# Linear attention with a gated convolution: q of four batches loaded in rows and in channels, with one set of PSUM tiles

## The chip, the cores and the metric

The kernel runs on one core of a Trainium2 chip. The metric is the device time in microseconds; it was measured in three runs of the kernel before. A profiled execution of the same program gives the trace. In the profile TensorE is called PE (its weight loads PEld), VectorE is DVE, ScalarE is ACT, GpSimd is POOL, and SyncE is SP; SP issues all DMAs of this kernel.

## The reference

There are 8 batches, 8 heads, 576 tokens and a head size of 64, so 512 channels; all data is float32.

```python
q_s = softmax(q, axis=-1)              # over the 64 channels of a head
k_s = softmax(k, axis=2)               # over the 576 tokens
kv  = einsum('bhsd,bhse->bhde', k_s, v)
x   = einsum('bhsd,bhde->bhse', q_s, kv)   # heads side by side: (8, 576, 512)

gate = sigmoid(sum over j of conv_w[j] * x shifted by 4 - j tokens)   # 5 taps
out  = (gate * (x @ w_val)) @ w_out
```

Both sums of a softmax get 1e-9 added before the division.

## The kernel before

The work goes batch by batch, and batches overlap. Channels are cut in 4 blocks of 128 (`NB`), and a block holds two heads. The tokens are 4 parts of 128 (`MAIN`, 512) and a tail of 64, which two batches share in one tile.

A list of named steps, `ORDER`, is written out by hand, as "name, batch, block or part, engine" (`a` ScalarE, `v` VectorE, `p` GpSimd). Each engine runs its instructions in the order of this list; nothing is reordered. A tile of a pool with n buffers waits for the release of an older one. The steps of one batch are:

- q: `load_q` brings the tokens on partitions, `q_max`, `q_sub`, `q_exp`, `q_sum` and `q_mul` make the softmax along the free axis. `q_turn` turns two blocks of 128 channels on TensorE (8 transposes of 128x128, line 445), `q_turned` copies them to SBUF; `tail_turn` and `tail_turned` do this for the shared tail (line 459). So q stands with its channels on partitions.
- k: `load_km`, `k_peak`, `k_row` (to DRAM) and `k_spread` (from DRAM to all partitions) give the maximum, `k_sub` and `k_exp` the exponential. Batches 0 and 1 take another way (`load_kc`, `k_top`, `k_raise`, `k_turn`).
- `kv` is the product over tokens (line 423), `kv_norm` divides by the sum of k, which comes from a column of ones at v.
- `attend b g` makes x for blocks 2g and 2g + 1 in two PSUM tiles (line 478), in pieces of 288, 224 and 64 tokens.
- `first` and four `tap` make the gate's sum from x in PSUM, on VectorE or on ScalarE and GpSimd together; `sigmoid` ends it. `x_high` and `x_low` split x into two rounded parts.
- `value b m` multiplies by w_val (24 matmuls of three terms: line 521), `gated` multiplies by the gate, `g_high` and `g_low` split again, `project b n` multiplies by w_out (line 521 again), `store` copies out of PSUM and sends it off.

The weights come as pairs of 32-bit words and are rebuilt at the start, in slabs: `load_words`, `part`, `field`, `scaled`, `signed`, `joined`, `w_high`, `w_low`. Slab i holds 128 output columns for all rows of the matrix, 0 to 3 of w_val, 4 to 7 of w_out, 8 the taps.

PSUM has two sets of two tiles, each of two banks: the tag `x` (for `attend`, `q_turn`, `q_lift`, `q_peak`) and the tag `mm` (the rest). The turned q has a tile of its own (`qT`), q itself two.

Of the kernel before, what the change touches and what calls it, by code (L numbers as in the profile page):

```python
# [23 lines left out]
KM = 3  # L24
EPS = 1e-9
MOST = 122880 - 2.0 ** -7
# [5 lines left out]
    load_q 0 0 2, load_words 1, q_max 0 0 2, load_ident, q_peak 0 0 2, load_words 8, part 8 a, field 1, scaled 1 a,  # L32
    signed 1, part 1 v, joined 1 p, w_high 1 p, field 8, scaled 8 a, q_top 0 0 2 a, load_kc 0 2, k_top 0 2,
    k_raise 0 2, q_lift 0 0, q_minus 0 0, w_low 1 p, load_q 0 2 5, q_lift 0 1, load_kc 0 1, q_max 0 2 5, k_top 0 1,
    load_kc 0 3, k_top 0 3, q_raise 0 0, k_raise 0 3, signed 8, q_peak 0 2 5, q_top 0 2 5 a, load_words 3, part 3 a,
    field 3, scaled 3 p, load_kc 0 0, k_top 0 0, load_q 1, signed 3, joined 3 p, k_turn 0 1, k_raise 0 0, q_minus 0 1,
    k_turned 0 1 a, q_raise 0 1, q_max 1, k_raise 0 1, load_words 4, field 4, w_high 3 p, scaled 4 a, load_kc 1 1,
    k_top 1 1, q_lift 0 2, q_minus 0 2, load_kc 1 0, k_top 1 0, k_turn 0 0, q_raise 0 2, k_raise 1 1, k_tail_turn 0,
    k_tail_turned 0 a, load_v 0, q_sum 0, signed 4, q_exps 1 1 p, q_exps 1 0 p, k_turned 0 0 a, q_exps 1 3 p,
    load_words 0, k_raise 1 0, field 0, q_exps 1 2 p, q_mul 0 1 v, scaled 0 p, joined 8 p, load_kc 1 2, k_top 1 2,  # L40
    load_words 2, q_sum 1, kv 0, field 2, q_mul 0 0 a, q_mul 0 2 a, q_mul 0 3 p, part 0 a, q_turn 0 0, q_turned 0 0 a,
    q_turn 0 1, q_turned 0 1 a, q_mul 0 4 p, kv_norm 0 a, load_kc 1 3, k_top 1 3, scaled 2 p, signed 2, tail_turn 0,
    tail_turned 0 a, attend 0 0, w_low 3 v, signed 0, part 2 a, joined 0 p, w_high 0 p, load_words 5, field 5,
    load_v 1, w_low 0 p, first 0 1 a, tap 0 1 3 v, first 0 0 a, x_high 0 0 a, k_raise 1 2, k_raise 1 3, k_turn 1 0,
    tap 0 1 2 v, k_turned 1 0 a, tap 0 0 3 v, load_words 6, tap 0 1 1 v, k_turn 1 1, tap 0 0 2 v, x_low 0 0,
    q_mul 1 2 p, k_turned 1 1 a, tap 0 0 1 v, tap 0 0 0 v, part 4 a, load_words 7, joined 2 p, joined 4 p,
    k_tail_turn 1, k_tail_turned 1 a, x_high 0 1 a, x_low 0 1, kv 1, tap 0 1 0 v, scaled 5 a, signed 5, kv_norm 1 v,
    sigmoid 0 0, q_mul 1 1 p, attend 0 1, load_k 3, part 5 a, x_high 0 2 a, joined 5 p, load_q 2, x_low 0 2, field 7,
    x_high 0 3 a, x_low 0 3, value 0 0, w_high 2 a, w_low 2 p, value 0 2, first 0 2 a, tap 0 2 3 v, w_high 4 a,
    w_low 4 p, load_kt 2, tap 0 2 2 v, q_mul 1 0 p, first 0 3 a, tap 0 3 3 v, load_km 2 1, gated 0 0, tap 0 2 1 a,  # L50
    load_km 2 2, scaled 7 a, tap 0 3 2 v, tap 0 3 1 v, tap 0 3 0 v, signed 7, k_peak 2 1, load_km 2 3, tap 0 2 0 a,
    q_mul 1 3 a, sigmoid 0 1, g_high 0 0 a, g_low 0 0 p, value 0 1, q_turn 1 0, k_peak 2 2, sigmoid 0 2, q_turn 1 1,
    load_km 2 0, gated 0 2, w_high 5 a, w_low 5 p, q_turned 1 0 a, g_high 0 2 a, part 6 a, g_low 0 2 p, gated 0 1,
    field 6, g_high 0 1 a, g_low 0 1 p, q_turned 1 1 a, load_k 2, load_v 2, value 0 3, q_max 2, q_sub 2 0 p,
    k_peak 2 3, k_peak 2 0, k_row 2, sigmoid 0 3, gated 0 3, attend 1 0, x_high 1 0 a, first 1 0 a, g_high 0 3 a,
    x_high 1 1 a, scaled 6 p, k_spread 2, first 1 1 a, signed 6, g_low 0 3 v, joined 6 p, w_high 6 a, q_sub 2 3 p,
    project 0 1, store 0 1 a, project 0 0, x_low 1 0, tap 1 1 3 v, w_low 6 p, project 0 2, tap 1 0 3 v, tap 1 1 2 v,
    tap 1 1 1 v, load_km 3 3, tap 1 0 2 v, part 7 a, tap 1 0 1 v, joined 7 p, tap 1 1 0 a, w_high 7 a, w_low 7 p,
    tap 1 0 0 v, sigmoid 1 0, x_low 1 1, load_km 3 2, store 0 2 a, load_km 3 0, k_peak 3 3, k_peak 3 2, store 0 0 a,
    attend 1 1, x_high 1 2 a, x_low 1 2, load_km 3 1, x_high 1 3 a, x_low 1 3, load_q 3, first 1 2 a, tap 1 2 3 v,  # L60
    tap 1 2 2 v, tap 1 2 1 v, q_sub 2 1 p, tap 1 2 0 v, first 1 3 a, q_sub 2 4 p, tap 1 3 3 v, k_peak 3 1, k_peak 3 0,
    project 0 3, store 0 3 a, k_sub 2 2 p, value 1 0, gated 1 0, k_sub 2 1 p, q_sub 2 2 p, sigmoid 1 1, q_exp 2,
    g_high 1 0 a, q_sum 2, k_sub 2 0 p, k_sub 2 4 p, k_sub 2 3 p, k_exp 2, value 1 1, gated 1 1, value 1 2, load_v 4,
    q_mul 2 0 a, q_mul 2 4 p, q_mul 2 1 p, tap 1 3 2 v, tap 1 3 1 v, load_km 4 0, tap 1 3 0 v, k_row 3, k_spread 3,
    kv 2, kv_norm 2 v, g_low 1 0 v, g_high 1 1 v, q_mul 2 2 a, g_low 1 1 v, sigmoid 1 2, q_mul 2 3 p, q_turn 2 0,
    q_turned 2 0 a, gated 1 2, g_high 1 2 p, load_km 4 1, k_peak 4 1, g_low 1 2 p, q_turn 2 1, q_turned 2 1 a,
    k_sub 3 2 p, load_km 4 2, load_v 3, k_sub 3 1 v, k_peak 4 2, value 1 3, sigmoid 1 3, gated 1 3, load_km 5 2,
    tail_turn 2, tail_turned 2 a, attend 2 0, g_high 1 3 a, g_low 1 3 p, load_km 4 3, x_high 2 1 a, k_sub 3 3 p,
    first 2 1 a, x_high 2 0 a, k_sub 3 0 p, q_max 3, q_sub 3 3 p, k_peak 4 3, first 2 0 a, tap 2 0 3 v, k_sub 3 4 p,
    tap 2 0 2 a, tap 2 0 1 a, tap 2 1 3 v, q_sub 3 0 p, x_low 2 1, project 1 3, store 1 3 v, x_low 2 0, k_exp 3,  # L70
    tap 2 1 2 v, tap 2 1 1 v, tap 2 1 0 v, tap 2 0 0 a, k_peak 4 0, k_row 4, k_spread 4, q_sub 3 1 p, project 1 0,
    load_km 5 3, store 1 0 v, project 1 1, store 1 1 a, q_sub 3 2 p, attend 2 1, x_high 2 3 a, x_low 2 3,
    x_high 2 2 a, load_k 4, first 2 2 a, tap 2 2 3 a, q_exp 3, first 2 3 v, k_peak 5 2, tap 2 3 3 v, kv 3,
    tap 2 3 2 v, tap 2 3 1 a, tap 2 3 0 a, load_q 4, kv_norm 3 v, project 1 2, store 1 2 a, x_low 2 2, q_sum 3,
    q_mul 3 3 p, q_mul 3 1 p, value 2 0, tap 2 2 2 v, sigmoid 2 0, tap 2 2 1 v, gated 2 0, g_high 2 0 v, load_km 5 1,
    q_mul 3 2 a, value 2 1, sigmoid 2 1, gated 2 1, load_km 6 3, q_mul 3 0 p, g_low 2 0 v, tap 2 2 0 a, q_turn 3 0,
    sigmoid 2 2, g_high 2 1 p, g_low 2 1 p, q_max 4, q_sub 4 2 p, q_sub 4 0 p, q_turn 3 1, q_turned 3 1 a, value 2 2,
    q_sub 4 4 p, gated 2 2, g_high 2 2 p, g_low 2 2 p, q_turned 3 0 a, attend 3 0, x_high 3 1 a, x_high 3 0 v,
    first 3 0 a, k_peak 5 1, load_q 5, load_k 6, tap 3 0 3 v, load_km 7 0, x_low 3 0, x_low 3 1, sigmoid 2 3,
    value 2 3, gated 2 3, g_high 2 3 v, first 3 1 a, g_low 2 3 v, k_peak 6 3, load_kt 4, k_sub 4 4 p, tap 3 0 2 a,  # L80
    tap 3 0 1 a, q_sub 4 1 p, tap 3 0 0 a, tap 3 1 3 v, k_sub 4 3 p, tap 3 1 2 v, tap 3 1 1 v, tap 3 1 0 v,
    load_km 5 0, project 2 0, store 2 0 v, q_sub 4 3 v, project 2 1, attend 3 1, first 3 2 v, first 3 3 v,
    x_high 3 2 a, k_peak 5 3, tap 3 3 3 v, store 2 1 a, load_km 6 2, tap 3 2 3 v, project 2 2, project 2 3,
    sigmoid 3 1, tap 3 2 2 v, k_sub 4 1 v, tap 3 2 1 v, x_low 3 2, x_high 3 3 a, x_low 3 3, store 2 2 a, k_sub 4 2 p,
    k_sub 4 0 v, q_exp 4, value 3 1, tap 3 2 0 a, q_sum 4, q_mul 4 3 p, q_mul 4 2 p, store 2 3 a, q_mul 4 0 p,
    k_exp 4, gated 3 1, sigmoid 3 0, value 3 0, k_peak 6 2, tap 3 3 2 a, gated 3 0, g_high 3 0 a, tap 3 3 1 a,
    k_peak 5 0, k_row 5, g_high 3 1 a, value 3 2, g_low 3 1 p, q_max 5, q_sub 5 1 p, tap 3 3 0 v, q_sub 5 2 p,
    q_mul 4 1 a, sigmoid 3 2, gated 3 2, load_km 6 0, k_peak 6 0, kv 4, kv_norm 4 v, q_turn 4 0, g_low 3 0 v,
    sigmoid 3 3, q_turn 4 1, q_turned 4 1 v, q_sub 5 3 p, k_spread 5, q_mul 4 4 p, value 3 3, gated 3 3,
    q_turned 4 0 a, q_sub 5 0 p, g_high 3 3 p, g_high 3 2 a, g_low 3 3 p, g_low 3 2 v, tail_turn 4, tail_turned 4 a,  # L90
# [549 lines left out]
```

## Time and profile before

| what | us |
| --- | --- |
| median of 3 runs | 311.24 |
| lowest and highest run | 308.35, 311.43 |
| the profiled execution | 309.28 |
| its span, first to last instruction | 307.5 |
| TensorE busy | 287.0 |
| VectorE busy | 247.3 |
| ScalarE busy | 207.4 |
| GpSimd busy | 187.7 |

The profile's page gives the busy time of each engine, its groups of instructions by line and what ended the idle time ahead of them, the chain of work that ended last, and the transfers with their time from issue to landing. Times within the execution count from the start of the span.

### The profile page before, as it was taken

To read this page: it belongs to the slowest core of one execution; us is meant where nothing else is said; L and a number is where in the kernel's file an instruction comes from. 1 tells how busy PE (TensorE), PEld (TensorE's weight loads), DVE (VectorE), ACT (ScalarE), POOL (GpSimd) and SP (SyncE) were. 2 spreads that over 40 slices of the span, in tenths; PEclk is the share of its full clock that TensorE was granted. 3 is DMA by queue.
4 is the path that set the end of the run, shared out by engine and by line. 5 is a ranking of instruction groups with operands and counts; after the bars stand their busy time and mean duration, and the time that the engine had idled before them with its cause. 6 is when DMAs were issued, how large, how long until landed. Compare 5 with 4: busy or idle time off the path is not lost.

```text
span 307.5 us, 6827 instructions
## 1 busy us (share of the span) xinstructions
PE 287.0 (93%) x2769; PEld 266.5 (87%) x2769; DVE 247.3 (80%) x338; ACT 207.4 (67%) x338; POOL 187.7 (61%) x163
## 2 busy tenths in 40 slices
...
GB/s 216 394 387 381 117 335 80 221 211 285 350 180 164 41 263 337 312 87 117 45 215 319 288 123 226 173 175 108 45 3 19 100 40 2 13 104 41 0 46 109
DMA packets 20527, 51.28 MB, mean 167 GB/s; under 512 B 2832, under 2 KB 7312, under 8 KB 17808
## 3 DMA queue, kind: packets, MB, share of 16 engines
...
## 4 chain that ended last, share of the span: by engine, by line
PE 59%; DMA 13%; ACT 8%; DVE 7%; POOL 6%; issue 4%; SPq 1%; ACTq 0%; DVEq 0%; POOLq 0%
PE out L521 21%; PE val L521 21%; PE kv L423 5%; DMA q<-in_q_tail 4%; PE x L478 3%; DMA km<-in_k_strided 3%; PE qTps L445 3%; DMA v<-in_v 3%; DMA out<-o 2%; DVE gate L503 2%; PE qlps L401 2%; DMA ident<-in_ident 2%; POOL q L346 2%; POOL gl L550 2%; PE qlps L406 2%
## 5 line engine op out<-in xcount | busy, mean ns | idle before, releaser
L521 PE MATMUL val<-x,w_val_hi 128*128 128x288 f32 x512 | 88.9, 295 | 0.0
L507 POOL TENSOR_TENSOR gate<-gate,far 128x572 f32<-128x572 f32 (+3 forms) x38 | 51.0, 1345 | 47.2 <-ACT far L506 46.2
L521 PEld LDWEIGHTS val<-x,w_val_hi 128*128 128x128 f32 x512 | 75.4, 188 | 0.0
L503 DVE SCALAR_TENSOR_TENSOR gate<-x,cw,gate 128x574 f32<-128x574 f32 (+3 forms) x90 | 71.7, 809 | 3.5 <-ACT gate L491 2.0
L521 PE MATMUL out<-gh,w_out_lo 128*128 128x288 f32 x256 | 56.9, 301 | 0.0
L521 PE MATMUL out<-gl,w_out_hi 128*128 128x288 f32 x256 | 56.0, 297 | 0.9 <-DVE gl L550 0.6
L521 PE MATMUL val<-x,w_val_lo 128*128 128x288 f32 x256 | 56.2, 301 | 0.0
L521 PE MATMUL out<-gh,w_out_hi 128*128 128x288 f32 x256 | 55.4, 295 | 0.0
L521 PEld LDWEIGHTS out<-gl,w_out_hi 128*128 128x128 f32 x256 | 41.4, 188 | 2.0 <-DVE gl L550 1.2
L521 PEld LDWEIGHTS out<-gh,w_out_lo 128*128 128x128 f32 x256 | 41.1, 188 | 1.0 <-DVE o L158 0.3
L506 ACT ACTIVATE far<-x,cw 128x572 f32<-128x572 f32 (+3 forms) x38 | 27.2, 736 | 21.8 <-DVE gate L503 16.5
L521 PEld LDWEIGHTS out<-gh,w_out_hi 128*128 128x128 f32 x256 | 41.6, 188 | 0.0
L521 PEld LDWEIGHTS val<-x,w_val_lo 128*128 128x128 f32 x256 | 40.9, 188 | 0.5
L542 DVE TENSOR_TENSOR g<-val,gate 128x576 f32<-128x576 f32 x32 | 23.9, 749 | 14.5 <-PE val L521 8.4
L156 ACT COPY o<-out 128x576 f32<-128x576 f32 (+1 forms) x23 | 14.2, 618 | 21.2 <-PE out L521 18.5
L510 ACT ACTIVATE gate<-gate 128x576 f32<-128x576 f32 x32 | 21.4, 684 | 10.6 <-DVE gate L503 6.9
L379 POOL TENSOR_TENSOR q<-q,qs 128x512 f32<-128x512 f32 x23 | 23.6, 1045 | 8.0 <-DVE qs L359 8.0
L497 DVE TENSOR_TENSOR x<-x,x 128x576 fp32r<-128x576 f32 x32 | 23.4, 751 | 4.9 <-ACT x L156 3.7
L342 DVE TENSOR_REDUCE qm<-q 128x32 f32<-128x2048 f32 (+3 forms) x9 | 20.5, 2279 | 8.1 <-DMA q<-in_q 4.8
L423 PE MATMUL kv<-v,k 128*64 128x65 f32 x512 | 22.0, 238 | 4.0 <-ACT k L156 2.7
L491 ACT ACTIVATE gate<-x,cw 128x576 f32<-128x576 f32 x24 | 17.7, 747 | 11.0 <-DVE x L497 3.9
L346 POOL TENSOR_TENSOR q<-q,qm 128x512 f32<-128x512 f32 x22 | 23.7, 1089 | 2.3 <-DVE qm L342 2.3
...
## 6 DMA issues: line engine op xcount, KB each, us to landing
...
v<-in_v SPq DMA_DIRECT2D x8, 1040.0 KB, 9.9
q<-in_q SPq DMA_DIRECT2D x7, 1024.0 KB, 7.7
...
k<-in_k SPq DMA_DIRECT2D x6, 1024.0 KB, 7.7
...
words<-in_w_val SPq DMA_DIRECT2D x4, 512.0 KB, 8.1
words<-in_w_out SPq DMA_DIRECT2D x4, 512.0 KB, 9.0
```

The lines of the kernel that those rows point to most:

```text
L342: nc.vector.tensor_reduce(out=T["qm", b][:, cs], in_=qq, axis=AX.X, op=ALU.max, negate=(b == 1))
L346: engine(e).tensor_sub(qq, qq, T["qm", b][:, cs].unsqueeze(2).broadcast_to([P, H, D]))
L379: engine(e).tensor_mul(qq, qq, s.unsqueeze(2).broadcast_to([P, H, D]))
L423: nc.tensor.matmul(acc[h * D:(h + 1) * D, p, :], T["k", b][:, c, cs] if c < 4 else ktz[b % 2][:, cs], T["v", b][:, c, hd] if c < 4 else T[ ...
L491: nc.scalar.activation(a, x, AF.Copy, scale=w)
L497: nc.vector.tensor_sub(xl, T["x", b, p], T["xh", b, p].bitcast(F32))
L503: nc.vector.scalar_tensor_tensor(out=a, in0=x, scalar=w, in1=a, op0=ALU.mult, op1=ALU.add)
L506: nc.scalar.activation(part, x, AF.Copy, scale=w)
L507: nc.gpsimd.tensor_add(a, a, part)
L510: nc.scalar.activation(T["gate", b, p], T["gate", b, p], AF.Sigmoid)
L521: nc.tensor.matmul(ps[:, cs], a[:, kb, ms], z[kb][:, cs], start=(kb == 0 and i == 0), stop=(kb == NB - 1 and i == 2),)
L542: nc.vector.tensor_mul(T["g", b, m], T["val", b, m], T["gate", b, m])
```

## The change

For batches 4 to 7, q is loaded twice. `load_qa` brings it in rows: a partition holds 36 rows (`ROWS`) of 64 channels, of one head each. `qa_max`, `qa_sub` (four pieces of 9 rows), `qa_exp` and `qa_sum` make the sum of the exponentials there, `qa_log` its logarithm plus the maximum. `q_row` sends these to DRAM, and two `q_spread` bring each head's row back to the 64 partitions of its channels. `load_qT` brings q with its channels on partitions; `q_add` subtracts the row, one block at a time, and `q_up` takes the exponential of two blocks. `q_turn`, `tail_turn` and `q_mul` go for these batches. `attend` takes their tokens in two pieces of 288 (`b >= EARLY`).

All q tiles, turned or not, share one tag of four buffers (`Q`). The turned tail takes a buffer of the tag `o`. PSUM has one set of four tiles. w_val is loaded by rows (slab i holds 128 rows of the matrix, all 512 columns), while w_out keeps its slabs of columns. `value` may come in two halves of the sum over blocks, which the four of batch 0 do. The step `signed` is cut in `shifted` and `signed`, and `field` may go to GpSimd. `ORDER` is new throughout, with other engines for some steps: 97 `tap` on VectorE and 31 on ScalarE with GpSimd (90 and 38 before).

```diff
-    psum = ctx.enter_context(tc.tile_pool(name="psum", bufs=2, space=PSUM))
-    def bank(name, tag="mm"):
-        return psum.tile([P, 2 * 512], F32, tag=tag, name=name)
+    psum = ctx.enter_context(tc.tile_pool(name="psum", bufs=4, space=PSUM))
+    def bank(name):
+        return psum.tile([P, 2 * 512], F32, tag="ps", name=name)
...
+    def q_tile(name):
+        return big.tile([P, 5 * C], F32, tag="q", name=name, bufs=Q)
...
+        elif i < NB:
+            nc.sync.dma_start(out=T["words", i], in_=w_val[:, i].rearrange("p (c t) -> p c t", t=2))
...
+    def load_qa(b):
+        T["qa", b] = q_tile(f"qa_{b}")[:, :ROWS * D]
+        nc.sync.dma_start(out=T["qa", b], in_=qa[b])
+    def load_qT(b):
+        nc.sync.dma_start(out=q_across(b), in_=qc[b])
+    def qa_max(b):
+        T["qm", b] = small.tile([P, 5 * H], F32, tag="qm", name=f"qm_{b}")[:, :ROWS]
+        nc.vector.tensor_reduce(out=T["qm", b], in_=by_row(b), axis=AX.X, op=ALU.max)
+    def qa_sub(b, i, e="p"):
+        ts = slice(ROWS // 4 * i, ROWS // 4 * (i + 1))
+        x = by_row(b)[:, ts]
+        engine(e).tensor_sub(x, x, T["qm", b][:, ts].unsqueeze(2).broadcast_to([P, ROWS // 4, D]))
+    def qa_exp(b):
+        nc.scalar.activation(T["qa", b], T["qa", b], AF.Exp)
+    def qa_sum(b):
+        s = T["qs", b] = small.tile([P, 5 * H], F32, tag="qs", name=f"qs_{b}")[:, :ROWS]
+        nc.vector.tensor_reduce(out=s, in_=by_row(b), axis=AX.X, op=ALU.add)
+        nc.vector.tensor_scalar_add(s, s, EPS)
+    def qa_log(b):
+        s = T["qs", b]
+        nc.scalar.activation(s, s, AF.Ln)
+        nc.vector.tensor_add(s, s, T["qm", b])
+    def q_row(b):
+        t = T["qrow", b] = rowpool.tile([H * S], F32, tag=f"qrow{b}", name=f"qrow{b}")
+        nc.sync.dma_start(out=t.rearrange("(p j) -> p j", j=ROWS), in_=T["qs", b])
+    def q_spread(b, half):
+        if ("qw", b) not in T:
+            T["qw", b] = q_tile(f"qw_{b}")[:, :NB * S].rearrange("p (n s) -> p n s", n=NB)
+        to = T["qw", b][half * D:(half + 1) * D].rearrange("p n s -> p (n s)")
+        r = T["qrow", b].rearrange("(o t m) -> o t m", o=1, t=2)[:, half]
+        nc.sync.dma_start(out=to, in_=r.broadcast_to([D, NB * S]))
+    def q_add(b, n, e="p"):
+        x = T["qT", b][:, n]
+        engine(e).tensor_sub(x, x, T["qw", b][:, n])
+    def q_up(b, g):
+        x = T["qT", b][:, 2 * g:2 * g + 2]
+        nc.scalar.activation(x, x, AF.Exp)
...
-        for t0, t1 in ((0, HALF), (HALF, MAIN), (MAIN, S)):
+        for t0, t1 in ((0, HALF), (HALF, MAIN), (MAIN, S)) if b < EARLY else ((0, HALF), (HALF, S)):
...
-    def value(b, m):
-        T["val", b, m] = halved_bank(f"val_{b}_{m}")
-        split_product(T["val", b, m], W[0], blocks("xh", b), blocks("xl", b), m)
+    def value(b, m, g="a"):
+        if ("val", b, m) not in T:
+            T["val", b, m] = halved_bank(f"val_{b}_{m}")
+        ks = range(NB) if g == "a" else (2 * g, 2 * g + 1)
+        z = [[T.get((x, b, k)) for k in range(NB)] for x in ("xh", "xl")]
+        split_product(T["val", b, m], W[0], *z, m, ks=ks)
```

From the new `ORDER`: its start, the first `value`, the chain of q for batch 7, and the end.

```diff
+    load_q 0 0 2, load_words 8, load_ident, q_lift 0 0, load_words 1, part 1 a, q_max 0 0 2, field 1 v, scaled 1 a,
+    field 8 p, scaled 8 p, load_words 3, field 3 v, scaled 3 a, shifted 1 v, part 8 a, signed 1, shifted 3 v,
...
+    load_v 1, kv 1, kv_norm 1 a, load_k 3, tap 0 1 2 v, tap 0 1 1 v, tap 0 1 0 v, attend 0 1, x_high 0 2 a,
+    first 0 2 a, x_low 0 2, load_q 3, tap 0 2 3 v, load_kt 2, first 0 3 a, x_high 0 3 a, x_low 0 3, w_low 0 p,
+    w_low 2 p, value 0 0 0, value 0 0 1, w_low 4 p, tap 0 2 2 v, tap 0 3 3 v, load_q 2, part 5 a, tap 0 2 1 v,
...
+    gated 5 3, g_high 5 3 v, g_low 5 3 v, g_high 5 0 p, g_low 5 0 p, k_spread 7, qa_log 7, q_row 7, kv 6, kv_norm 6 v,
+    q_up 6 0, project 5 3, q_spread 7 0, k_sub 7 0 v, attend 6 0, x_high 6 1 a, k_sub 7 1 v, first 6 1 a, project 5 2,
+    store 5 3 a, project 5 0, k_sub 7 4 v, first 6 0 v, tap 6 0 3 v, k_sub 7 3 v, k_sub 7 2 v, tap 6 0 2 a, k_exp 7,
+    tap 6 1 3 v, tap 6 1 2 a, store 5 2 v, q_add 6 3 v, q_spread 7 1, tap 6 0 1 v, kv 7, q_add 6 2 v, x_high 6 0 v,
+    q_up 6 1, store 5 0 a, x_low 6 0, tap 6 0 0 v, kv_norm 7 v, attend 6 1, first 6 2 a, tap 6 1 1 v, tap 6 1 0 a,
+    first 6 3 v, tap 6 3 3 v, tap 6 3 2 a, x_high 6 2 a, x_low 6 1, project 5 1, store 5 1 a, q_add 7 2 v, x_low 6 2,
+    x_high 6 3 a, tap 6 2 3 v, tap 6 2 2 a, sigmoid 6 1, x_low 6 3, q_add 7 0 v, q_add 7 3 v, value 6 1, gated 6 1,
...
+    gated 7 3, g_high 7 3 v, g_low 7 3 v, project 7 0, store 7 0 a, project 7 1, store 7 1 v, project 7 3 r,
+    project 7 2, store 7 2 v, store 7 3 a r, project 7 3 l, store 7 3 a l,
```

More of the change, by code (lines that the diff above doesn't have):

```diff
@@ L24 @@
 KM = 3
+GATES = 6
+PAIRS = 6
+Q = 4
+ROWS = S // 16
 EPS = 1e-9
+EARLY = 4
 MOST = 122880 - 2.0 ** -7
 ORDER = [step.strip() for step in """
[L32 to L90, printed above, removed]
@@ L101 @@
-    q_turn 5 0, q_turned 5 0 a, q_sub 6 2 p, q_exp 6, load_q 7, g_high 4 0 p, g_low 4 0 v, value 4 3, load_kt 6,
-    gated 4 3, g_low 4 1 v, g_high 4 3 p, g_low 4 3 p, attend 5 0, x_high 5 1 v, x_low 5 1, k_peak 7 3, k_sub 6 4 p,
-    first 5 0 a, tap 5 0 3 a, project 4 0, store 4 0 a, first 5 1 a, q_max 7, x_high 5 0 v, x_low 5 0, load_k 7,
-    tap 5 1 3 a, tap 5 1 2 a, tap 5 1 1 a, tap 5 1 0 a, tap 5 0 2 v, project 4 1, store 4 1 a, project 4 3,
-    store 4 3 a, tap 5 0 1 v, tap 5 0 0 v, sigmoid 5 0, attend 5 1, first 5 3 a, tap 5 3 3 a, x_high 5 2 a,
@@ new lines @@
+    scaled 7 a, q_turned 1 0 a, load_km 2 1, k_peak 2 1, load_k 2, g_low 0 2 p, tap 0 3 0 v, sigmoid 0 3, w_low 5 p,
+    load_words 6, part 6 a, field 6 p, k_peak 2 2, gated 0 1, g_high 0 1 a, q_max 2, value 0 3 0, value 0 3 1,
+    scaled 6 a, gated 0 3, attend 1 0, g_low 0 1 p, shifted 6 v, x_high 1 0 a, shifted 7 v, signed 6, g_high 0 3 a,
+    g_low 0 3 p, load_km 2 0, k_peak 2 0, first 1 0 a, tap 1 0 3 v, x_high 1 1 a, load_v 3, q_turn 1 1,
+    q_turned 1 1 a, load_km 2 3, load_km 3 1, x_low 1 1, tap 1 0 2 v, project 0 0, project 0 1, store 0 0 a,
@@ new lines @@
+    x_low 1 0, joined 6 p, w_high 6 a, q_sub 2 2 p, w_low 6 p, k_peak 2 3, project 0 2, first 1 1 a, tap 1 1 3 v,
+    signed 7, part 7 a, joined 7 p, tap 1 0 1 v, q_sub 2 1 p, load_km 3 2, k_row 2, tap 1 1 2 v, store 0 1 a,
+    tap 1 0 0 v, w_high 7 a, w_low 7 p, k_spread 2, tap 1 1 1 v, q_sub 2 0 p, attend 1 1, tap 1 1 0 a, x_high 1 3 a,
+    x_high 1 2 a, first 1 2 a, tap 1 2 3 a, load_km 3 3, q_max 3, x_low 1 3, store 0 2 a, q_sub 2 3 v, k_peak 3 1,
+    sigmoid 1 1, x_low 1 2, q_sub 2 4 p, load_v 2, project 0 3, k_sub 2 3 p, k_peak 3 2, tap 1 2 2 v, first 1 3 a,
@@ new lines @@
+    project 1 1, attend 2 1, kv 3, load_km 6 0, k_peak 4 3, x_high 2 3 a, k_peak 4 1, x_low 2 3, load_v 4,
+    first 2 2 a, store 1 1 v, x_high 2 2 a, x_low 2 2, kv_norm 3 v, q_sub 3 3 p, q_sub 3 2 p, project 1 2, q_exp 3,
+    q_sum 3, load_km 6 1, tap 2 2 3 a, sigmoid 2 0, qa_max 4, q_mul 3 0 p, first 2 3 a, tap 2 3 3 a, tap 2 2 2 v,
+    tap 2 3 2 a, k_row 4, load_km 6 2, store 1 2 a, tap 2 2 1 v, value 2 0, gated 2 0, tap 2 2 0 v, k_peak 6 2,
+    q_mul 3 3 p, tap 2 3 1 v, tap 2 3 0 v, value 2 1, g_high 2 0 p, g_low 2 0 p, k_spread 4, q_mul 3 1 a, q_mul 3 2 a,
```

172 lines of the change are left out of this document (109 added, 63 removed).

## The prediction

> **What bounds the kernel now.** I read the page's busy table first, then the work by stretch of time, the chain that ended last, and TensorE's waits.
>
> ```profile
> span 307.5 us, 6827 instructions
> ...
> PE 287.0 (93%) x2769; PEld 266.5 (87%) x2769; DVE 247.3 (80%) x338; ACT 207.4 (67%) x338; POOL 187.7 (61%) x163
> ```
>
> TensorE (PE) is busy 93% of the span. That is an average over two stages, so I cut the span where the first product of the gated half begins. The stretches give, for each engine, busy time (instructions), then the granted clock, the DMA share and GB/s:
>
> ```profile
> core 0: us, PE busy (x) PEld busy (x) DVE busy (x) ACT busy (x) POOL busy (x), PEclk, DMA share, GB/s
> 0.00:44.00 44.00, 30.18 (x289) 19.99 (x293) 34.86 (x53) 33.03 (x64) 25.06 (x28) 0.92 0.86 314
> ...
> 44.00:304.40 260.40, 256.83 (x2488) 246.51 (x2480) 212.46 (x286) 174.00 (x275) 162.68 (x135) 1.00 0.42 142
> 140.00:304.40 164.40, 162.12 (x1570) 156.42 (x1569) 125.66 (x168) 102.89 (x156) 86.10 (x72) 1.00 0.30 105
> ```
>
> Before 44 us TensorE is idle 44.00 - 30.18 = 13.8 us, while VectorE (DVE), ScalarE (ACT) and the transfers are loaded: the start hangs on them. After 44 us TensorE is idle 260.40 - 256.83 = 3.6 us in all, at full clock. Nothing else comes near: DVE has 260.4 - 212.5 = 47.9 us to spare there, ACT 86.4, GpSimd (POOL) 97.7. The chain, with start and length in us, agrees at its two ends:
>
> ```profile
> 43.12 1.14 PE x L478 x24
> 44.26 9.90 PE val L521 x72
> ...
> 291.54 12.79 PE out L521 x96
> 304.34 0.40 ACT o L156
> ```
>
> So the time is the start of the first `value` (44.3), TensorE's work from there (256.8), its idle time (3.6), and the last store with its DMA (307.5 - 304.3 = 3.2). An edit counts by which of the four it moves. The profiled execution took 309.28 us for its span of 307.5, 1.8 us outside; the median of the runs, 311.24, is 2.0 above it.
>
> **The change part by part.**
>
> *Transposes of q, batches 4 to 7.* They go: eight `q_turn` of 8 transposes, two `tail_turn` of 4. Restricted to line 445, the last stretch shows exactly the 64 that go:
>
> ```profile
> 140.00:304.40 164.40, 8.40 (x64) 7.20 (x64) 1.00 0.30 105
> ```
>
> Busy times overlap at their ends, so I take the step from start to start in the timeline (start, us, instruction):
>
> ```profile
> 219.00 1.03 PE L445 MATMUL qTps<-ident,q 128*128 128x128 f32 x8
> 219.88 0.60 PE L459 MATMUL qTtps<-ident,q 128*128 128x128 f32 x4
> 220.23 0.51 PE L521 MATMUL val<-x,w_val_lo 128*128 128x288 f32 x2
> ```
>
> One `q_turn` costs 219.88 - 219.00 = 0.88, one `tail_turn` 0.35. Eight and two: 7.0 + 0.7 = 7.7 us, and 8.40 + 2 x 0.60 = 9.6 at most, by busy time. TensorE is nearly never idle here, so this is on the path.
>
> *`attend` in two pieces of tokens.* In batches 4 to 7 the pieces 288, 224 and 64 become 288 and 288, so 16 instructions instead of 24:
>
> ```profile
> 230.36 1.09 PE L478 MATMUL x<-qT,kvd 64*64 64x288 f32 x16
> 231.27 0.29 PE L478 MATMUL x<-qTt,kvd 64*64 64x64 f32 x8
> 231.49 0.53 PE L521 MATMUL out<-gh,w_out_lo 128*128 128x288 f32 x2
> ```
>
> The first 512 columns take 0.91 us, the 64 of the tail 0.22. At the rate of the former, 64 columns more cost 0.91 x 64/512 = 0.11: saved 0.11 in each of eight, 0.9 us; bounds 0 and 8 x 0.22 = 1.8. TensorE's work falls by 7.7 + 0.9 = **8.6 us** (bounds 7.7 and 11.4). Splitting the first four `value` in halves adds no matmul.
>
> *What the other engines get instead.* The groups of instructions (busy us, mean ns of one) price it:
>
> ```profile
> L156 ACT COPY qT<-qTps 128x1024 f32<-128x1024 f32 x15 | 14.7, 1008 | 2.0 <-PE qTps L445 1.8
> L377 ACT ACTIVATE q<-q,qs 128x64 f32<-128x64 f32 x80 | 19.9, 340 | 0.4 <-DVE qs L359 0.4
> L350 ACT ACTIVATE q<-q 128x2560 f32<-128x2560 f32 (+1 forms) x6 | 12.8, 2134 | 0.1
> L491 ACT ACTIVATE gate<-x,cw 128x576 f32<-128x576 f32 x24 | 17.7, 747 | 11.0 <-DVE x L497 3.9 <-PE x L478 3.6 <-DVE x L158 3.4
> L156 ACT CAST x<-x 128x576 fp32r<-128x576 f32 x26 | 16.2, 643 | 9.2 <-PE x L478 5.9 <-DVE gate L493 2.8 <-DVE gate L503 0.4
> L503 DVE SCALAR_TENSOR_TENSOR gate<-x,cw,gate 128x574 f32<-128x574 f32 (+3 forms) x90 | 71.7, 809 | 3.5 <-ACT gate L491 2.0
> L497 DVE TENSOR_TENSOR x<-x,x 128x576 fp32r<-128x576 f32 x32 | 23.4, 751 | 4.9 <-ACT x L156 3.7 <-ACT far L506 1.0
> L236 DVE TENSOR_SCALAR e<-words 128x512 f32<-128x512 f32 x8 | 3.4, 430 | 1.3 <-DMA words<-in_w_val 1.3
> L346 POOL TENSOR_TENSOR q<-q,qm 128x512 f32<-128x512 f32 x22 | 23.7, 1089 | 2.3 <-DVE qm L342 2.3
> L550 POOL TENSOR_TENSOR gl<-g,gh 128x576 fp32r<-128x576 f32 x16 | 23.2, 1452 | 2.9 <-ACT gh L156 2.2
> ```
>
> DVE gains 8 `q_add` like line 497 (6.0) and 7 `tap` (5.7), 11.7, and loses two `g_low`, three `k_sub`, four `q_sub`, two stores and others of 0.4 to 1.2 us, about as much. POOL gains 14 `qa_sub` of 576 columns (14 x 1.089 x 576/512 = 17.2) and 8 `q_add` like line 550 (11.6) for 12 `q_mul` and 14 `q_sub`. ACT gains 8 `q_up` of 1152 columns (8 x 1.008 x 1152/1024 = 9.1); four `qa_exp` stand for four `q_exp` of the 2.1 us row. It loses 7 copies of `qT` (7.1) and 32 of the 80 small multiplications (32 x 0.249 = 8.0). Even with nothing subtracted, the 11.7, 28.8 and 9.1 us lie within the 47.9, 97.7 and 86.4 to spare. I cost them at nothing; TensorE's queue covers them, and where an engine is late just ahead of an `attend`, it shows as idle time below.
>
> *ACT's tables.* There are 16 loads now (four groups, of 8, 5, 2 and 1), one at the start and one at each change between exponential and sigmoid: walking the old order gives the same 16. One takes 1.28 us (row below). The new order gives 20 if `qa_log` is served by the exponential's table, 27 if not: 5.1 to 14.1 us more. The chain shows no load on the path, so I price neither end into the sum and take the dear one as ACT's burden: still far below 86.4. [...]
>
> ```profile
> 41.65 1.28 ACT L510 ACT_TABLE_LOAD   x1
> 42.94 0.68 ACT L510 ACTIVATE gate<-gate 128x576 f32<-128x576 f32 x1
> ```
>
> The activation starts at 42.94, 0.01 after the load's end.
>
> *The new chain of q.* Each of the four batches now passes a row through DRAM (`q_row`), two broadcasts of 590 KB to 64 partitions each (`q_spread`), `q_add`, `q_up`. Landing times of the nearest transfers (KB each, median us):
>
> ```profile
> v<-in_v SPq DMA_DIRECT2D x8, 1040.0 KB, 9.9
> q<-in_q SPq DMA_DIRECT2D x7, 1024.0 KB, 7.7
> kmax<-krow SPq DMA_DIRECT2D x6, 256.0 KB, 4.7
> words<-in_w_val SPq DMA_DIRECT2D x4, 512.0 KB, 8.1
> ```
>
> Between 256 KB in 4.7 and 1024 KB in 7.7, 590 KB takes 4.7 + 3.0 x 334/768 = 6.0 us (bounds 4.7 and 9.9). By the new order, TensorE has this to do between the issue of the second `q_spread` and the first `q_add`, at 3.2 us for a `value` or `project`, 2.5 for a `kv`, 1.1 for an `attend`: batch 4, three `value`, 9.6; batch 5, `attend`, `kv`, `value`, 6.8; batch 6, two `value`, 6.4; batch 7, `kv`, `attend`, `project`, 6.8. A 6.0 with 0.4 for the issue just fits. Behind a late `q_add 7 2` on DVE stand `x_low 6 2` and `x_low 6 3`, for which `value 6 1` waits; in batches 5 and 6 it is POOL that would wait. SP issues its DMAs in order, so a `q_spread` that waits for its tile or its row holds the loads of k and v behind it; they are placed more than a batch ahead. In bytes, four times 3.5 MB replace 4.7 MB: 9.4 MB more in a stretch whose DMA share is 0.30, which they lift to about 0.5.
>
> *PSUM in one set of four, the new waits.* TensorE's own waits after 44 us (us, times, longest):
>
> ```profile
> PE x L478 <- ACT far L506: 0.9, 1, 0.9
> PE kv L423 <- DMA v<-in_v: 0.9, 1, 0.9
> PE out L521 <- DVE gl L550: 0.6, 1, 0.6
> ```
>
> Only the first is a wait for a PSUM tile. What the one set and the new order do to the 3.6 us of idle time no row tells: from -3.6 (all gone) to +9 (below). I take +2.0, one wait of the size of these, 0.5 us, for each batch with the new chain.
>
> *The start.* By the order, DVE does less ahead of the first `value`: three `field`, one each of shift, `signed`, `w_low` and `part` fewer, one `tap` more, 2.7 us by their rows of 0.4 to 0.8. ACT does 0.5 less, since a table load, a sigmoid and a `q_mul` go and three `w_high` and two `first` come. Against this, all four rows of w_val must be ready by the second half instead of one slab, and two transfers of words are ahead of the rest of q (1.0 MB, 2.7 us at some 390 GB/s). I take **1.0 us** earlier, between -2.7 and +2.7. The words of w_val (8.1 us to landing above) now come in runs of 4 KB, not 1 KB; I cost that at nothing, since DVE and ACT, not these words, end last at 44 us.
>
> **Sum**: 309.28 - 8.6 - 1.0 + 2.0 = 301.7 on the profiled execution's footing. The runs shown lie at or up to 2 us above it; I add half of the 2.0 and an even figure is **302.5 us**.
>
> **The rivals.**
>
> *More comes back (295).* The start gains DVE's whole 2.7, and the new order uses up the 3.6 of idle time: 309.28 + 1.0 - 8.6 - 2.7 - 3.6 = 295.4. For it: ACT is unloaded too. Against it: something always ends last at the start.
>
> *The row through DRAM lands late (311).* At the 9.9 us of `v`, with 0.4 for the issue, batches 5 and 7 are 3.5 late, 6 is 3.9, 4 about 1.2; half of it in 5 and 6, where POOL waits, is covered: 3.5 + 1.2 + 3.7 = 8.4, so 302.5 + 8.4 = 310.9. For it: broadcasts read the same 9 KB 64 times. Against it: DMA share 0.30. [...] No row here has 64 partitions at this size.
>
> *TensorE starves for PSUM tiles (318, slower).* With one set, the second `attend` of a batch may take the two tiles that `value` and `project` had for themselves, and then TensorE stands until the seven readers of an x tile are done: about 5.4 us (two ACT passes of 0.7, five DVE ones of 0.8), against 3.2 for a product. One us at each of 16 `attend` is 16: 302.5 + 16 = 318. It decides from 0.75 us at each: 12 us, past 314.4. Against it: the 0.9 above, with sets of two.
>
> **How the numbers follow.** Forecast 0.60 (its own range 298 to 306), more back 0.12, late rows 0.18, starved 0.10. A measurement of this kernel tells 1%, or 308.1 and 314.4, from no change. Faster: 0.60 + 0.12 + a third of the late rows, 0.78; same 0.14 with the rest of these and mild starving; slower 0.08. The range 294 to 311.5 takes in the forecast, the better case and half of the late rows.
>
> **What would show it.** Right: after the first `value` TensorE's busy time falls to about 248 with 5 to 6 us idle; only 64 `qTps` transposes left; the first `value` near 43. Wrong: DVE or POOL waiting for `qw` from DRAM; `x` matmuls waiting on readers for microseconds; a first `value` after 46; table loads ahead of `q_up` on the chain.

## The result, and the profile after

The changed kernel takes 296.02 us (median of 4 runs, 294.41 to 298.67) against 309.80 for the kernel before beside it (306.64 to 311.43): a ratio of 0.960 with a 95% interval of 0.947 to 0.973. The same kernel, run twice more, gave 296.38 (ratio 0.960, 0.951 to 0.969) and 295.74 (0.959, 0.953 to 0.965). The forecast was 302.5 in a range of 294 to 311.5, so sign and range held; the gain was 13.8 us where about 8 were forecast. The ratios leave out executions over 1.5% longer than the fastest of the same kernel, the medians take in all.

The busy table of the changed kernel, to set beside that of before:

```profile
span 292.5 us, 6556 instructions
...
PE 276.6 (95%) x2633; PEld 253.8 (87%) x2633; DVE 247.3 (85%) x337; ACT 214.1 (73%) x316; POOL 181.7 (62%) x157
```

VectorE's sum is the same 247.3 as before; only the span around it is shorter. TensorE lost 10.4 us of busy time, yet its share rose: the rest of the gain is time in which it did nothing. The work by stretch of time, same columns as before, with the last stretch ending where the last product ends:

```profile
core 0: us, PE busy (x) PEld busy (x) DVE busy (x) ACT busy (x) POOL busy (x), PEclk, DMA share, GB/s
0.00:44.00 44.00, 32.40 (x305) 20.83 (x306) 33.44 (x51) 32.93 (x61) 25.86 (x30) 0.96 0.89 332
44.00:140.00 96.00, 95.40 (x925) 91.30 (x924) 92.10 (x123) 79.42 (x135) 75.40 (x65) 1.00 0.69 224
140.00:289.40 149.40, 148.76 (x1407) 141.67 (x1406) 121.73 (x165) 101.72 (x123) 80.43 (x64) 1.00 0.50 163
```

After 44 us TensorE is idle 0.6 + 0.6 = 1.2 us, where it was 3.6; half of the 1.2 lies behind its last matmul. The chain that ended last says the same. From 70 us on it is nearly TensorE alone, with no gap between one row's end and the next row's start:

```profile
149.46 2.48 PE kv L443 x80
151.94 3.39 PE val L592 x24
155.33 1.13 PE x L549 x16
156.46 13.00 PE out L592 x96
169.46 1.13 PE x L549 x16
170.59 2.48 PE kv L443 x80
```

TensorE's own waits confirm it. After 40 us three are left, 1.0 us in all (columns: us, times, longest):

```profile
PE val L592 <- issue: 0.4, 1, 0.4
PE out L592 <- POOL w_out_lo L278: 0.4, 1, 0.4
PE val L592 <- DVE x L568: 0.2, 1, 0.2
```

Put together over the two profiled executions: the first `value` starts at 42.4 instead of 44.2 (-1.8), the stretch from there to the end of the last product is 246.4 instead of 260.1 (-13.7), the tail is 3.8 instead of 3.1 (+0.6). The span falls by 14.9, from 307.45 to 292.55.

To split the 13.7 I took each matmul's step from its start to the next one's start, less any gap, and summed by product. Transposes for q went from 13.4 to 5.6 us (-7.8). The products `value`, `project` and `kv` and the matmuls of `attend` went from 242.9 to 239.9 (-3.1) at the same counts, except for `attend`, whose 336 became 272. Gaps went from 3.5 to 0.6 (-2.9).

### The profile page after: what moved, and what is told of

It reads as the page before. It is cut to its first block, busy times and chain, and to the rows that moved or that the text cites. A ratio compares the mean times of both kernels' runs of the same rounds, so it can differ in the third digit from the quotient of the medians.

```text
span 292.5 us, 6556 instructions
## 1 busy us (share of the span) xinstructions
PE 276.6 (95%) x2633; PEld 253.8 (87%) x2633; DVE 247.3 (85%) x337; ACT 214.1 (73%) x316; POOL 181.7 (62%) x157
## 4 chain that ended last, share of the span: by engine, by line
PE 76%; ACT 11%; DVE 4%; issue 3%; DMA 2%; POOL 1%; SPq 1%; ACTq 0%
PE out L592 33%; PE val L592 31%; PE kv L443 5%; PE x L549 5%; DMA q<-in_q 2%; ACT kc L327 1%; PE qTps L465 1%; PE qlps L421 1%; ACT q L397 1%; DVE gate L574 1%; ACT f L169 1%; ACT gate L562 1%; ACT k L163 1%; ACT x L163 1%; DVE kpk L290 1%
## 5 line engine op out<-in xcount | busy, mean ns | idle before, releaser
L574 DVE SCALAR_TENSOR_TENSOR gate<-x,cw,gate 128x575 f32<-128x575 f32 (+3 forms) x97 | 77.0, 808 | 2.9 <-ACT gate L562 1.3
L578 POOL TENSOR_TENSOR gate<-gate,far 128x574 f32<-128x574 f32 (+3 forms) x31 | 41.9, 1354 | 41.0 <-ACT far L577 40.0
L592 PE MATMUL val<-x,w_val_lo 128*128 128x288 f32 x256 | 55.5, 298 | 0.4 <-issue 0.4
L592 PE MATMUL out<-gl,w_out_hi 128*128 128x288 f32 x256 | 55.4, 295 | 0.0
L624 POOL TENSOR_TENSOR gl<-g,gh 128x576 fp32r<-128x576 f32 x18 | 25.6, 1429 | 15.9 <-ACT gh L163 13.6
L163 ACT COPY o<-out 128x576 f32<-128x576 f32 (+1 forms) x25 | 15.6, 623 | 21.2 <-PE out L592 12.8
L577 ACT ACTIVATE far<-x,cw 128x574 f32<-128x574 f32 (+3 forms) x31 | 22.1, 740 | 8.8 <-DVE gate L574 6.5
L568 DVE TENSOR_TENSOR x<-x,x 128x576 fp32r<-128x576 f32 x32 | 23.8, 750 | 1.8 <-ACT x L163 1.2
L305 POOL TENSOR_TENSOR k<-k,kmax 128x512 f32<-128x512 f32 x19 | 24.2, 1288 | 0.1
L163 ACT CAST x<-x 128x576 fp32r<-128x576 f32 x24 | 15.1, 643 | 8.7 <-PE x L549 8.6
L443 PE MATMUL kv<-v,k 128*64 128x65 f32 x512 | 19.6, 224 | 1.7 <-ACT k L163 1.7
```

The source lines that it names most:

```text
L163: nc.scalar.copy(out=out, in_=in_)
L305: engine(e).tensor_sub(kk[r, cs], kk[r, cs], mx[r, cs])
L443: nc.tensor.matmul(acc[h * D:(h + 1) * D, p, :], T["k", b][:, c, cs] if c < 4 else ktz[b % 2][:, cs], T["v", b][:, c, hd] if c < 4 else T[ ...
L568: nc.vector.tensor_sub(xl, T["x", b, p], T["xh", b, p].bitcast(F32))
L574: nc.vector.scalar_tensor_tensor(out=a, in0=x, scalar=w, in1=a, op0=ALU.mult, op1=ALU.add)
L577: nc.scalar.activation(part, x, AF.Copy, scale=w)
```

## The experiments

The theory after the result: TensorE has no slack, so (a) the transposes count in full, and (b) each turning also held a PSUM tile until ScalarE had copied it, which delayed `attend` and the products around it; the new order with one set of tiles is laid out without those tiles. What else `ORDER` changed (engines of some steps, halves of `value`) isn't separated from (b). The rivals: the one set alone gives the gain; the earlier start or the loading of w_val by rows gives it; the table loads or the row through DRAM still cost something that hides the rest.

**TensorE's work alone (e1).** In the changed kernel, for batches 4 to 7:

```diff
+            if b >= EARLY:
+                for i in range(8 if b % 2 == 0 and m == 0 else 4):
+                    nc.tensor.transpose(T["val", b, m][:, (i % 2) * P:(i % 2 + 1) * P], ident, ident)
```

These 72 transposes write into banks that `value` overwrites, so no tile and no copy comes with them.

> The changed kernel, with 72 transposes of the identity (as many as the change took away) put back as bare TensorE work: they go into the PSUM tile of a value just before its first matmul overwrites it, so no tile, no copy and no wait comes back with them. If TensorE's queue is the bound after the first value, all of their 7.7 us comes back: span 292.5 + 7.7 = 300.2 us, about 304 in the runs, ratio 0.985. If the change gained by waits that went with the turning, and TensorE has slack, less than 3 us comes back: span under 295.5.

Measured 304.45 us, ratio 0.985 (0.980 to 0.990), 8.4 above the changed kernel. From the first `value` to the start of the last matmul it takes 253.9 us against 246.1: 7.8 more, as much as the transposes that went. The window over that stretch shows that they came on top, with TensorE still never idle for more than 0.7 us in all:

```profile
45.50:299.80 254.30, 253.61 (x2412) 242.39 (x2412) 215.17 (x289) 182.59 (x259) 157.46 (x129) 1.00 0.54 180
```

So (a) holds, and it gives a little over half of the gain. With all of that work back, the stretch is still 5.9 us shorter than in the kernel before.

**Work and copies, still no PSUM tile (e8).** As e1, and beside it a ScalarE copy of the same size from one spare SBUF tile to another where each turning was.

```diff
+    def again(b, g):
+        n = 8 if g < 2 else 4
+        nc.scalar.copy(out=spare[1][:, :n * P], in_=spare[0][:, :n * P])
```

> The changed kernel with the 72 bare transposes and, at the places of the turning put back whole, the ScalarE copies of 1024 (512) columns, but from SBUF to SBUF, so that no PSUM tile is taken. The bare transposes cost 8.4 us in the runs, the turning put back whole 19. If the copies (9.3 us of ScalarE) make the difference, this is near the whole turning: over 310 us. If the PSUM tile held from the transposes to the copy's end makes it, this is near the bare transposes: 303 to 306 us.

Measured 303.91 us, ratio 0.988 (0.983 to 0.993): the same as e1. From the first `value` to the last matmul it takes 255.3 us, 8.1 more than the changed kernel beside it (247.2). The copies cost nothing that can be seen.

**The turning put back whole (e2).** The same transposes and copies, now through a PSUM tile of their own, one product ahead of each `attend`:

```diff
+    def again(b, g):
+        ps = bank(f"again_{b}_{g}")
+        n = 8 if g < 2 else 4
+        for i in range(n):
+            nc.tensor.transpose(ps[:, i * P:(i + 1) * P], ident, ident)
+        nc.scalar.copy(out=work.tile([P, 8 * P], F32, tag="again", name=f"again_{b}_{g}s")[:, :n * P], in_=ps[:, :n * P])
```

> The changed kernel, with the turning of batches 4 to 7 put back whole as dead work, one product ahead of each attend: a PSUM tile, 8 transposes (4 for the tail), a copy of 1024 (512) columns on ScalarE. If the gain beyond TensorE's work (some 6 us) came from the new order and the set of four, this costs like the bare transposes, 7.7 to 9 us: span 300 to 302. If that part came from the tiles and copies of the turning, it costs 12 to 14 us: span 305 to 307, the time of before.

Measured 315.01 us, ratio 1.020 (1.009 to 1.031): slower than the kernel before. From the first `value` to the start of the last matmul it takes 262.0 us against 246.1: 8.2 of transposes, 6.3 more gaps and 1.5 inside the other products. That is 8.1 more than e1 and 6.7 more than e8, which has as many transposes and copies; the medians of e2 and e8 lie 11 apart, but the start, which differs from run to run, is in them. TensorE's waits after 44 us name the copy that frees the tile twice, and exponentials of ScalarE that come late beside it:

```profile
PE kv L452 <- ACT k L318: 1.5, 1, 1.5
PE x L565 <- ACT qT L533: 1.4, 2, 1.0
PE out L608 <- ACT again_1s L540: 1.2, 1, 1.2
PE kv L452 <- ACT again_1s L540: 1.2, 1, 1.2
```

So (b) holds for this order: put through a PSUM tile ahead of `attend`, the turning costs 15.9 us, about twice its transposes. e8 and e2 differ in the tile, and with it in where the transposes stand (there spread over the `value`, here together) and in what the copies wait for; which of these weighs most wasn't separated. The 7 to 8 us are not the price in the old order, which was laid out around such tiles and lost only 3.5 us to gaps in its whole stretch; of TensorE's waits there, only 0.3 us stand ahead of a turning.

**One set under the old order (e4).** The kernel before with only its PSUM changed:

```diff
-    psum = ctx.enter_context(tc.tile_pool(name="psum", bufs=2, space=PSUM))
+    psum = ctx.enter_context(tc.tile_pool(name="psum", bufs=4, space=PSUM))
-        return psum.tile([P, 2 * 512], F32, tag=tag, name=name)
+        return psum.tile([P, 2 * 512], F32, tag="ps", name=name)
```

> The kernel before, with one set of four PSUM tiles as the only edit. If the set by itself removes waits, the 3 to 6 us of them go: span 302 to 305. If the order has to be made for it, within 1.5 us of 307.5. By the rival of my prediction that a common set starves TensorE, slower: span over 310.

Measured 308.27 us, ratio 1.002 (0.997 to 1.007): no change. Its one profile has the stretch from the first `value` 2.3 us shorter than the profile of the kernel before, 1.3 of it in gaps; two profiles of the changed kernel lie 1.1 apart there. One set gives nothing by itself that the times show.

**Two sets under the new order (e3).** The changed kernel with the old tags for its PSUM tiles. The new order holds three tiles of one old set at seven places, so 13 steps (`tap`, `x_low`, `gated` and a `sigmoid`) are moved ahead there.

```diff
-    psum = ctx.enter_context(tc.tile_pool(name="psum", bufs=4, space=PSUM))
+    psum = ctx.enter_context(tc.tile_pool(name="psum", bufs=2, space=PSUM))
-    def bank(name):
-        return psum.tile([P, 2 * 512], F32, tag="ps", name=name)
+    def bank(name):
+        tag = "x" if name.startswith(("x_", "qlps", "qpk")) else "mm"
+        return psum.tile([P, 2 * 512], F32, tag=tag, name=name)
```

> The changed kernel with two sets of two PSUM tiles as before (x tiles of attend, q_lift and q_peak in one, all others in the other). Eleven readers are moved ahead of the step that would need a third tile of a set, else the order is the new one. If the one set of four is what removed the waits, TensorE waits again at the seven places where the order holds three tiles: 4 us or more, span 296.5 to 300. If the order and the missing turning did it, less than 1.5 us: span 292 to 294.

Measured 335.0 us, ratio 1.087 (1.081 to 1.094). Now TensorE waits for the readers of PSUM tiles, which is what the prediction's third rival described, but through two sets and not through one:

```profile
PE x L549 <- DVE gate L574: 6.9, 3, 2.5
PE val L592 <- DVE g L616: 5.7, 4, 1.8
PE x L549 <- DVE x L568: 2.6, 1, 2.6
```

Of the 39 us above the changed kernel, 15.0 lie ahead of the first `value` (57.3 us), where no step was moved; there TensorE also ran at the slow pace of which the last section tells (0.94 to 1.04 us for a matmul of 512 columns, up to 27.6 us). From the first `value` to the last matmul it is 25.7 more, 16.1 of it in gaps. With e4 this suggests that order and set belong together: the order uses tiles as one set lets it. How much is the moved readers and how much the sets can't be told from this run.

**No logarithm (e5).** The cost of the dearer count of table loads; this kernel leaves the logarithm out, and with it 7 of the 27 loads:

```diff
-        nc.scalar.activation(s, s, AF.Ln)
+        nc.scalar.copy(out=s, in_=s)
```

> The changed kernel, which loads 27 tables on ScalarE, with a copy in place of the logarithm; this leaves the logarithm out of the computation and with it the 7 table loads that the four of them cause, 9.0 us of ScalarE. If ScalarE is covered by TensorE's queue, as the prediction had it, within 1 us of the changed kernel. If table loads delay q_up and the sigmoids on the path, 3 to 9 us faster.

Measured 297.66 us, ratio 0.959 (0.947 to 0.971): no difference from the changed kernel (296.38 beside it). The loads are covered, as costed.

**Each q_spread twice (e6).** How near the row through DRAM is to being late:

```diff
-        nc.sync.dma_start(out=to, in_=r.broadcast_to([D, NB * S]))
+        for _ in range(2):
+            nc.sync.dma_start(out=to, in_=r.broadcast_to([D, NB * S]))
```

> The changed kernel with every q_spread issued twice into the same place, so that the rows land some 5 us later (5.3 us one, the second behind it). By the prediction's margins of 6.4 to 9.6 us, POOL and DVE now wait at q_add for the row in each of four batches, 2 to 4 us each: 4 to 10 us slower in all. If the chain has more slack than that sum says, less than 2 us.

Measured 330.41 us, ratio 1.064 (1.053 to 1.076): 34 more, far above what any theory had said. The waits of SP's queue show why. The second issue of each pair goes to the same tile and stands in the queue until the first has landed:

```profile
SPq L517 <- DMA qw<-qrow: 44.4, 8, 6.6
```

So beside the doubled bytes, this run has a delay of some 11 us in each of four batches. What it delays is seen in the waits of GpSimd and VectorE, and TensorE's behind them:

```profile
POOL qT L521 <- DMA qw<-qrow: 33.8, 3, 14.3
DVE qT L521 <- DMA qw<-qrow: 9.2, 1, 9.2
PE x L550 <- ACT qT L525: 14.8, 2, 8.1
```

43.0 us of lateness became 23.8 us more of gaps on TensorE. Another 9 us are the same products taking longer: `value` and `project` took 106.2 and 108.5 us instead of 104.1 and 104.3, `attend` 19.1 instead of 16.6. A lower granted clock goes with it in some windows (the last three columns are granted clock, DMA share, GB/s); how much of the 9 us it makes wasn't worked out:

```profile
156.00:164.00 8.00, 4.84 (x74) 4.54 (x70) 0.43 (x1) 2.88 (x3) 0.00 (x0) 1.00 0.65 152
164.00:172.00 8.00, 3.08 (x20) 1.84 (x21) 6.34 (x10) 2.47 (x4) 2.54 (x2) 0.58 0.76 279
```

After 3.2 us of standing in one window the granted clock of the next, in which TensorE stands 4.9 us, is 0.58. The windows from 204 and 244 us, with stands of 5.0 and 3.2 us, have 0.64 and 0.70. The changed kernel has 1.00 in all of this stretch.

**Each q_spread twice, the second into a tile that nobody reads (e10).** The bytes without the delay:

```diff
+        nc.sync.dma_start(out=spare[half * D:(half + 1) * D], in_=r.broadcast_to([D, NB * S]))
```

> The changed kernel with every q_spread issued a second time, this time into a tile that nobody reads. The bytes and the issues are those of the experiment that issued each one twice into its own tile (330 us, where the second issue of each pair stood in SP's queue until the first had landed: 8 waits, 44.4 us). If that one was slow because the rows came some 12 us later: here nothing waits for a landing, the transfers stand side by side, landing may grow from 5.3 to 6 to 8 us, and the time stays within 2 us of the changed kernel, 295 to 298. [...]

Measured 305.73 us, ratio 0.984 (0.977 to 0.992); the changed kernel beside it took 295.74. So it is 10.0 us slower, and the expectation of at most 2 us is out. The transfers of this kernel (KB each, median us to landing):

```profile
qT<-in_q_channels SPq DMA_DIRECT2D x4, 1152.0 KB, 11.2
qw<-qrow SPq DMA_DIRECT2D x8, 576.0 KB, 5.6
spare<-qrow SPq DMA_DIRECT2D x8, 576.0 KB, 7.8
```

its waits for them:

```profile
SPq L300 <- DMA krow<-kpk: 25.8, 5, 12.5
POOL qT L521 <- DMA qw<-qrow: 9.4, 3, 6.9
```

and the landings of `qw`, first of the changed kernel, then of this one:

```profile
DMA to landing us min/median/max: 5.1/5.3/7.7
DMA to landing us min/median/max: 5.1/5.6/10.0
```

The medians hide the second `q_spread` of a batch. In the changed kernel it lands in 6.7 to 7.7 us where it is issued within 1.2 us of the first (three batches), else in 5.1. Here, in batch 4, four transfers issued within 1.9 us land at 152.3, 155.0, 157.9 and 161.0 us, one behind the other, and the second `q_spread` takes 9.1 to 10.0 us in three batches. Other transfers lag too: `qT` takes 11.2 instead of 6.9, and SP's wait for the row of k goes from 11.4 to 25.8 us in all. From the first `value` to the last matmul it costs 8.0 us, 4.2 in gaps and 3.6 in `kv` and `attend`. In its profiled execution (307.31) the first `value` also started 5.3 later than in the changed kernel beside it, of which the last section tells.

So the second transfers cost 8.0 us without the 44.4 us in SP's queue that e6 had. Two windows of this run show what the transfers take: in the first `qT` and k are on their way (128 partitions each), in the second mostly the rows (64 each):

```profile
196.00:204.00 8.00, 8.00 (x68) 7.22 (x67) 7.05 (x11) 6.49 (x9) 3.93 (x4) 1.00 1.03 411
212.00:220.00 8.00, 8.00 (x62) 8.00 (x61) 7.83 (x12) 7.78 (x9) 6.08 (x6) 1.00 0.96 234
```

With the queues about as full, the rows move 234 GB/s instead of 411. Whether the 64 partitions or the 64 reads of one row do this wasn't separated. The changed kernel has such stretches too, by windows of 20 us:

```profile
140.00:160.00 20.00, 20.00 (x218) 18.98 (x218) 17.76 (x24) 18.07 (x22) 9.72 (x8) 1.00 0.96 285
160.00:180.00 20.00, 20.00 (x219) 19.15 (x219) 18.49 (x26) 16.99 (x21) 18.84 (x16) 1.00 0.88 285
```

**w_val by slabs of columns (e7).** The loading and splitting of w_val put back as before:

```diff
-        elif i < NB:
-            nc.sync.dma_start(out=T["words", i], in_=w_val[:, i].rearrange("p (c t) -> p c t", t=2))
...
+            src = (w_val, w_out)[i // NB].rearrange("p k (c t) -> p k c t", t=2)
+            nc.sync.dma_start(out=to, in_=src[:, :, slab(i)])
```

> The changed kernel with w_val loaded and split by slabs of 288 columns as before, not by rows; the first four value stay in halves, so a half needs its own slabs alone. By the prediction's step (the start is set by DVE and ScalarE, not by these words): within 1 us of the changed kernel, first value within 1 us of 42.4. If loading by rows is what made the start earlier: first value at 43.5 to 45 and the time 1 to 2.5 us more. If rows only held the first value back, since all four must be there by the second half: 1 to 2 us less.

Measured 295.76 us, ratio 0.962 (0.955 to 0.969), first `value` at 42.7 us: no change.

**The changed kernel again (e0, twice).**

> The changed kernel once more, beside these. It shows how far a second profile's start of the first value lies from 42.4 us: the same code up to there began it at 45.5 and 45.0 in the two kernels with dead transposes. If the start of 42.4 belongs to the change, 42 to 43 again; if it varies from run to run, anywhere from 42 to 46, with the span moving as much and 246 us from the first value to the last product all the same.

> The changed kernel once more, on the chip of the three others, to compare them with. 295 to 297 us. If the first value begins again near 42.4 us (44.2 before), the earlier start is of the kernel; if it lies anywhere between 42 and 45, it is of the run.

296.38 and 295.74 us; first `value` at 42.4 and 42.5 us. With e7 that makes four profiles at 42.4 to 42.7, against 44.2 for the kernel before and 43.9 for e4, which has the old start too. But six other profiles with the steps of this start have 45.0 (e2), 45.5 (e1, e5), 47.8 (e10), 47.9 (e6) and 49.1 (e8).

**Batch 3 as well (e9).** `EARLY = 3`, with the steps of batch 3 exchanged in the order:

```diff
-EARLY = 4
+EARLY = 3
...
+    qa_exp 3, qa_sum 3, load_km 6 1, tap 2 2 3 a, first 2 3 a, qa_max 4, qa_log 3, q_row 3, sigmoid 2 0,
...
+    store 1 2 a, q_spread 3 1, q_spread 3 0,
...
+    q_add 3 0 p, q_add 3 1 v, q_add 3 2 p, sigmoid 2 1, k_peak 6 1, sigmoid 2 2, q_up 3 0, q_add 3 3 p,
```

> The changed kernel with the new form of q for batch 3 too (five batches by rows and channels, three still turned). Two q_turn of 0.88 us go (1.8 us of TensorE) and two PSUM tiles with their ScalarE copies; a fifth row through DRAM, two more q_spread and 0.6 MB more for each come, and four q_mul are replaced by a logarithm, two q_up and four q_add. If TensorE's work and the tiles held set the time, and the row is in time: 1.8 to 4 us less than the changed kernel, 292 to 294.5 us. If transfers are too dense around 120 to 135 us (the stretch is at some 220 GB/s already) or the row of batch 3 is late: no gain, or up to 8 us more, 296 to 304.

Measured 316.16 us, ratio 1.010 (1.002 to 1.018), outside both expectations; its best run, 309.77, is 14 above the changed kernel's median beside it. Its profiled execution ran at a granted clock of 0.56 throughout and took 449 us, so nothing is read from it, and why this version is slower stays open. The runs with more transfers (e10) and with a delayed row (e6) make a late row or a full queue likely; that is argued, not shown.

## Why the prediction was right, and where its size was off

Sign and path were right: TensorE's work and its idle time after the first `value` set the time, and the work that went came off in full. The forecast's own range, 298 to 306, was missed; 296.02 lies in the wider one because that took in the rival "more comes back". Of the signs named, the 64 transposes and a first `value` near 43 came; TensorE is busy 245.8 us after it and idle 0.6, not 248 and 5 to 6.

*Transposes, -7.7.* Measured -7.8, and e1 put 7.8 back with the work alone. None are left after 140 us, 48 are in the gated stretch (64 with the 16 ahead of it). This step held to 0.1 us, by its size and by its mechanism.

*`attend` in two pieces, -0.9.* Wrong: the chain before had "1.14 PE x L478 x24", now it is 1.13 for 16 instructions.

```profile
220.12 1.20 PE L549 MATMUL x<-qT,kvd 64*64 64x288 f32 x16
221.25 0.54 PE L592 MATMUL out<-gh,w_out_lo 128*128 128x288 f32 x2
```

The step is 221.25 - 220.12 = 1.13. The prediction took the tail's 0.22 us as dear for its 64 columns, since 512 had taken 0.91. Dropping the piece gave none of that back: 16 matmuls of 288 columns take as long as 24 of 288, 224 and 64, for the same columns in all. The saving is 0.007 us each, 0.06 in all, near the lower bound of 0 that the text had kept.

*New waits, +2.0.* The step that failed, and with the wrong sign: between -3.6 and +9, it was taken at +2.0. What the runs show in its place is -5.9: 2.9 of gaps that went, and 3.1 inside the products (less the 0.06 of `attend`), which were not visible as gaps. Four of the 14 `attend` after the first `value` took 1.4 to 1.9 us from start to start in the kernel before, where the other ten took 1.14 to 1.19; in the changed kernel one of 14 did (1.77). The ends of matmuls are modelled in the profile, so such waits can stand inside them. The prediction read 3.6 us as all that idle time could give, so even its own bound was too tight. It also put no price on the turning's PSUM tile: between e8 and e2, where the same turning goes without and with a tile, lie 6.7 us from the first `value` on. That shows the tile's price in the new order; which part of the 5.9 came from the tiles and which from the rest of the new order stays open. The rival "more comes back", at 295.4, had the size, by the start and the 3.6 us of visible idle time; that it came so close is partly luck.

*The start, -1.0.* It came 1.8 earlier in the profiles of this section, within the bounds of 2.7. But the same steps began the first `value` anywhere from 42.4 to 49.1 us, along with TensorE's pace in the start (last section), and the old start has two profiles, so how much the new order gives here stays open. The loading by rows, which the step held against the start, counts for nothing (e7).

*Other engines, nothing.* VectorE's sum did not move, ScalarE rose by 6.7 and GpSimd fell by 6.0 us. The table loads came in the dear count:

```profile
L581 ACT ACT_TABLE_LOAD x10 | 12.8, 1283 | 1.5 <-DVE gate L574 1.4
L524 ACT ACT_TABLE_LOAD x6 | 7.7, 1283 | 0.1
L504 ACT ACT_TABLE_LOAD x4 | 5.1, 1283 | 0.1
```

These and seven more make 27: `qa_log` (line 504) loads its own table each time and the next exponential (`q_up`, line 524, in three of four batches) loads another behind it, 1.28 us each, so logarithm and exponential did not share one here. e5 shows that it costs nothing either way: without seven of the loads it took 297.66 us, against 296.38.

*The row through DRAM.* The landing, estimated at 6.0, is 5.1 to 5.3 us for the first `q_spread` of a batch and 6.7 to 7.7 for one right behind it; nobody waits for it in the changed kernel:

```profile
qa<-in_q_rows SPq DMA_DIRECT2D x4, 1152.0 KB, 7.1
qT<-in_q_channels SPq DMA_DIRECT2D x4, 1152.0 KB, 6.9
qw<-qrow SPq DMA_DIRECT2D x8, 576.0 KB, 5.3
```

In e10 the rows land one behind the other and move 234 GB/s, against 411 for `qT` and k; whether that comes from their 64 partitions or from the 64 reads of one row was not shown. The rival's price was near the mark: it took landings at 9.9 us as worth 8.4, and e10, with 9.1 to 10.0 in three batches, costs 8.0. Its sum has a slip: by its own margins batch 4 is 10.3 - 9.6 = 0.7 late, not 1.2, which makes 7.9. e6 shows that 43 us of late rows turn into 24 of gaps and 9 more in slower products. The DMA share of "about 0.5" was right as a mean (0.50) and hid a first 40 us at 0.96 and 0.88.

*PSUM starving, 318.* Not in this kernel. The price was right in kind: TensorE did stand on the readers of x when the tiles were cut into two sets (e3: 6.9 and 2.6 us ahead of `attend`).
